# Attention and two MoE layers on one core: sums moved between engines, a shorter weight conversion, a new order

## The chip, the cores and the metric

One Trainium2 chip, one core. The metric is the device time of one execution in microseconds (us). A core has TensorE (PE in the profile), VectorE (DVE), ScalarE (ACT), GpSimd (POOL) and SyncE (SP), which here issues most DMAs. Each engine works through its own instructions in order and waits on semaphores.

## What is computed

Attention over q, k, v (batch 4, 8 heads, 576 tokens, 64 columns), then two feed-forward layers. Attention has two parts that are added:

```
q_d, k_d, v_d = mean over groups of 4 tokens            # 144 pooled tokens
out_up    = repeat(softmax(scale * q_d k_d^T) v_d, 4)   # pooled, for every token
out_local = softmax(where(|i - j| < 4, scale * q k^T, -1e9)) v
x = out_up + out_local                                  # 2304 tokens x 512
x = silu(x @ w_in) @ w_out                              # 512 -> 2048 -> 512
out = rational(x @ w_in2) @ w_out2                      # cubic over quadratic
```

Both softmaxes subtract the row's maximum and divide by the sum of the exponentials (+ 1e-9). The weights arrive as 64-bit floats, and the kernel converts them on the chip.

## The kernel before, in words

**Attention.** Each batch has five chunks of 116 or 112 tokens. A chunk's k and q, with a halo, come in one DMA (tile kq, six buffers), its v in another (vw). The local part of a chunk c of batch b is a row of jobs: S (scores with a band mask, L563, L572), M (maxima, L578), E (exponentials, L584 and eight L588), U (their sum L593, plus 1e-9 L594, reciprocal L595), N (scaling, L598, on VectorE or GpSimd), T (transposes, L609), C (copy to PT), O (times v, L629), A (add the pooled part, L636), H and X (split into a rounded half and a rest, L650). The pooled part runs in two halves: s, m, e (six L478), u (sum L483, reciprocal L484), n, t, c, o (L510), U. A needs its result, so the first chunk's x waits for the whole pooled part of its batch.

The sums over four tokens of q and k (tile kqd) and of v (vd) are made in two ways. In batch 0 five reductions on VectorE (job R, L399) read the kq tiles, and v comes in four strips (tile vst, L409) that GpSimd (L417, L418) or VectorE (L415) adds up. In batches 1 to 3 four DMAs per sum put the four tokens' parts on one another; the last three accumulate and are issued by GpSimd (L428, L435).

**The MoE layers.** The first layer runs in 80 steps: five blocks of some 460 tokens times 16 slices of the hidden width. Steps 0 to 7 are block 0 with slices 0 to 7, steps 8 to 23 block 1 with all slices, then the rest of block 0 and the other blocks. A step is twelve matmuls into the hidden layer (h_mm, L798), an activation (L961, L964, L334, L973), and twelve matmuls out of it (o_mm, L812). Each weight slice of both layers (64 pieces) is first converted by `piece`: 1 (absolute value of the high word, L710), 2 (the low word scaled, L714), 3 (clamp L717, then shift and mask L719), 4 (add, L723, on VectorE or GpSimd), 5 (sign and exponent, L726), 6 (rounded half), 7 (rest, L734). Steps 0 to 7 need 16 pieces, steps 8 to 15 none, steps 16 to 23 again 16; the second layer's 32 go to DRAM along the way. The second layer (from about 545 us) loads them back.

**The order.** Nothing is scheduled at run time. `Plan` holds every job of attention, conversion and the first layer with a due time, its cost on each engine that may do it, the jobs it comes after and the buffers it takes and gives back; `Plan.run` lists them by a simulation of the engines, latest start first, and each engine gets its instructions in that order. Jobs marked `port` don't run on VectorE and GpSimd at once. EARLY bounds how far ahead of its latest start a job may begin (50 us). `settle` repeats the simulation ROUNDS times with the start times that it found and keeps the best. While no MoE step has begun, gaps of TensorE are filled with matmuls that nothing reads (warm, L294).

Of the kernel before, what the change touches and what calls it, by code (L numbers as in the profile page):

```python
# [52 lines left out]
EARLY = 50000.0  # L53
ROUNDS = 6
WARM0 = 20
WARM0_END = 3800.0
# [20 lines left out]
class Job:  # L77
# [3 lines left out]
    def __init__(self, name, due, cost, emit, after=(), take=(), give=(), margin=0.0, size=0.0,  # L81
                 closes=False, early=EARLY, port=False, step=None):
        self.port = port
# [12 lines left out]
class Plan:  # L96


    LAT, OWN = 200.0, 90.0
    DMA_LAT = 2000.0  # L100
# [23 lines left out]
    def run(self, when):  # L124
# [20 lines left out]
        free = dict.fromkeys("PVAGD", 0.0)  # L145
        port = 0.0
# [4 lines left out]
        while events:  # L151
# [87 lines left out]
def v_ns(n):  # L239
    return 66 + 1.042 * n  # L240
# [10 lines left out]
def r_ns(n, count):  # L251

    return count * (n / 2.4 + 17)
# [3 lines left out]
def tile_kernel(ctx, tc, kq, kqs, vp, vw_in, moe_w_in, moe_w_out, moe2_w_in, moe2_w_out, moe2_a, moe2_b, out):  # L257
# [87 lines left out]
    E2_t = [at.tile([128, 6, SD + 1], F32, tag=f"EE{i}", name=f"EE{i}", bufs=1) for i in range(2)]  # L345
# [19 lines left out]
    for e in E2_t:  # L365
        nc.gpsimd.memset(e[:, :, SD:], 1e-9)
# [8 lines left out]
    def attention(b):  # L375
# [17 lines left out]
        vs = []  # L393
        if b == 0:
            for t in range(NCH):
                def sm(e, t=t):
                    o = kqd[:, :2 * KT * SD].rearrange("p (g s) -> p g s", g=2 * KT)[:, :, at0[t] // 4:(at0[t] + CHUNKS[t]) // 4]
                    i = kqt[t][:, :2 * KT * KW].rearrange("p (g s) -> p g s", g=2 * KT)[:, :, HALO:HALO + CHUNKS[t]]
                    nc.vector.tensor_reduce(out=o, in_=i.rearrange("p g (j r) -> p g j r", r=4), axis=AX.X, op=ALU.add)  # L399
                sums.append(plan.add(f"R{b}{t}", FAR, {"V": v_ns(8 * CHUNKS[t])}, sm, after=[loads[t]] + sums[:1],  # L400
                                     take=[] if sums else [kdu], give=[kqu[t]]))
            for i in range(2):
                for hf in range(2):
                    wn = 2 * i + hf + NF - 7
                    u = Unit(f"w{wn}")
                    st = {}
                    def lv(e, i=i, hf=hf, st=st, wn=wn):
                        st[0] = wp.tile([128, 4, 256], F32, tag=f"w{wn}", name="vst")[:HS]
                        nc.sync.dma_start(out=st[0], in_=vp[b, :, :, i, 256 * hf:256 * hf + 256].rearrange("r s c -> s r c"))  # L409
                    def pv(e, i=i, hf=hf, st=st):  # L410
                        if not vdt:
                            vdt[0] = at.tile([HS, 2, DM], F32, tag="vd", name="vd", bufs=1)
                        o = vdt[0][:, i, 256 * hf:256 * hf + 256]
                        if e == "V":
                            nc.vector.tensor_reduce(out=o, in_=st[0].rearrange("p r c -> p c r"), axis=AX.X, op=ALU.add)  # L415
                        else:
                            nc.gpsimd.tensor_tensor(out=st[0][:, 0:2], in0=st[0][:, 0:2], in1=st[0][:, 2:4], op=ALU.add)  # L417
                            nc.gpsimd.tensor_tensor(out=o, in0=st[0][:, 0], in1=st[0][:, 1], op=ALU.add)  # L418
                    l = plan.add(f"v{b}{i}{hf}", FAR, {"D": 60}, lv, take=[u], size=HS * 4096)
                    vs.append(plan.add(f"p{b}{i}{hf}", FAR, {"G": 2050, "V": 1950}, pv,  # L420
                                       after=[l] + vs[:1], take=[] if vs else [vdu], give=[u]))
        else:
            def ks(e, r):
                o = kqd[:, :2 * KT * SD]
                if r == 0:
                    nc.sync.dma_start(out=o, in_=kqs[b, r])
                else:
# [9 lines left out]
            for f, u, o, n, m in ((ks, kdu, sums, "K", 128 * 4608), (vsum, vdu, vs, "Q", HS * 4096)):  # L437
                j = None
                for r in range(4):
                    j = plan.add(f"{n}{b}{r}", FAR, {"G": 1000} if r else {"D": 60}, lambda e, f=f, r=r: f(e, r),  # L440
                                 after=[j] if j else takes[n], take=[] if j else [u], size=m, margin=500 if r else 0)
                    if r == 0:
                        takes[n] = [j]
                o.append(j)
        if b == 0:
            takes.update(K=sums[:1], Q=vs[:1])
# [4 lines left out]
        for m in range(2):  # L451
# [20 lines left out]
            def ex(e, x=x, eu=eu):  # L472
                x["e"] = E2_t[eu.no]
                nc.scalar.activation(x["n"], x["n"], AF.Copy, scale=D ** -0.5 / 16.0)
                for e_ in range(2):
                    for t in range(3):
                        i = 3 * e_ + t
                        nc.scalar.activation(x["e"][:, i, :SD], x["s"][:, e_, SD * t:SD * t + SD], AF.Exp,  # L478
                                             scale=D ** -0.5 / 16.0, bias=x["n"][:, i:i + 1])

            def su(e, x=x):
                x["r"] = at.tile([128, 6], F32, tag="r2", name="r2", bufs=3)
                nc.vector.tensor_reduce(out=x["r"], in_=x["e"], axis=AX.X, op=ALU.add)  # L483
# [47 lines left out]
            jo = plan.add(f"o{b}{m}", d0, {"P": 950}, pv2, after=pc + vs + ups[:1], take=[p3] + ([] if ups else [upu]), give=[pt, vdu],  # L531
                          margin=MARGIN if b else MARGIN0)
# [4 lines left out]
        for c in range(NCH):  # L537
# [44 lines left out]
            def ex(e, x=x, eu=eu):  # L582
                x["e"] = E_t[eu.no]
                nc.scalar.activation(x["n"], x["n"], AF.Copy, scale=D ** -0.5)  # L584
                for e_ in range(2):
                    for g in range(KT):
                        i = KT * e_ + g
                        nc.scalar.activation(x["e"][:, i], x["s"][:, e_, WK * g:WK * g + WK], AF.Exp,  # L588
                                             scale=D ** -0.5, bias=x["n"][:, i:i + 1])

            def su(e, x=x):
                x["r"] = at.tile([128, 8], F32, tag="r1", name="r1", bufs=4)
                nc.vector.tensor_reduce(out=x["r"], in_=x["e"], axis=AX.X, op=ALU.add)  # L593
# [58 lines left out]
            if i == 0:  # L652
# [4 lines left out]
            js = plan.add(f"S{b}{c}", d0, {"P": 1000}, s, after=[loads[c]], take=[pS, eu], give=[kqu[c]],  # L657
                          margin=MARGIN if b else MARGIN0)
            jm = plan.add(f"M{b}{c}", d0, {"V": v_ns(8 * WK)}, mx, after=[js])
            je = plan.add(f"E{b}{c}", d0, {"A": 8 * (a_ns(WK) + 93) + 200}, ex, after=[jm], give=[pS])  # L660
            ju = plan.add(f"U{b}{c}", d0, {"V": v_ns(8 * WK) + 270}, su, after=[je])
            jn = plan.add(f"N{b}{c}", d0, {"V": v_ns(8 * WK), "G": 130 + 1.72 * 8 * WK}, no, after=[ju], port=True)
            jt = plan.add(f"T{b}{c}", d0, {"P": 530}, tr, after=[jn], take=[pT] + ([] if b == 0 and c == 4 else [pt]), give=[eu],
                          margin=MARGIN if b else MARGIN0)
            jc = plan.add(f"C{b}{c}", d0, {"A": a_ns(8 * sub), "V": v_ns(8 * sub)}, cp_, after=[jt] + (c3 if b == 0 and c == 4 else []), give=[pT])
            c3 = [jc]
            jo = plan.add(f"O{b}{c}", d0, {"P": 770}, pv, after=[jc, jl] + ups, take=[pO, xu], give=[pt, vu],
                          margin=MARGIN if b else MARGIN0)
# [7 lines left out]
    takes = {}  # L676
# [13 lines left out]
    def piece(name, due, src, dst, home, after=None):  # L690
# [485 lines left out]
```

## Time and profile before

| | us |
|---|---|
| median of 3 runs | 924.31 (923.57 to 924.56) |
| the profiled execution, its time | 927.42 |
| its span, first to last instruction | 925.6 |
| TensorE busy | 898.1 |
| VectorE busy | 721.8 |
| ScalarE busy | 597.9 |
| GpSimd busy | 333.7 |
| granted TensorE clock, mean | 0.993 |

The profile is of one execution. A line as L717 is a line of the kernel before. A busy TensorE is not TensorE at its peak, since matmuls are pipelined and their ends modelled; so below its work is also counted in matmuls.

### The profile page before, as it was taken

The page shows a single profiled execution, that of the slowest core. Times are in us where ns is not written, and L with a number is a line of the kernel's source. Part 1 is how long each engine was busy: PE and PEld are TensorE (multiplying, and loading weights), DVE is VectorE, ACT ScalarE, POOL GpSimd, SP SyncE. Part 2 cuts the span into 40 slices and gives each one's busy share as a digit, 9 for nine tenths or more (in the row PEclk, how much of TensorE's full clock was granted, in tenths as well). Part 3 has the DMA queues.
Part 4 walks back from the last instruction along what each step waited for, and adds up shares of the span by engine and source line. Part 5 has one row for each costly group of instructions (what it writes and reads, how often), then busy time and mean ns, then how long its engine had stood idle before and what let it go on. Part 6 is the DMA issues. An engine that isn't in the chain of part 4 may idle for free.

```text
span 925.6 us, 15469 instructions
## 1 busy us (share of the span) xinstructions
PE 898.1 (97%) x5885; PEld 759.2 (82%) x5885; DVE 721.8 (78%) x1054; ACT 597.9 (65%) x1179; POOL 333.7 (36%) x271
## 2 busy tenths in 40 slices
PE   7898999999999999999999999999999999999997
PEld 5676788867887788888888878888888888898996
DVE  7998995997458757886322289998998899799995
ACT  5867664766447746664222378888777877788874
POOL 4532231523124312110000146565554555455553
PEclk9998999999999999999999999999999999999999
DMA  8997897788889787879864091002001100200000
GB/s 263 309 268 242 262 280 240 277 265 247 266 241 315 255 275 255 277 279 322 272 233 159 10 393 48 1 1 91 1 1 43 38 0 1 80 1 1 35 1 35
DMA packets 48614, 152.36 MB, mean 165 GB/s; under 512 B 5308, under 2 KB 10556, under 8 KB 48540
## 3 DMA queue, kind: packets, MB, share of 16 engines
q1 hardware_dynamic: 45548, 142.46, 44.4%
q0 software_dynamic: 2704, 8.91, 5.6%
q8 instruction: 46, 0.75, 0.3%
q14 instruction: 28, 0.23, 0.1%
q10 hardware_dynamic: 288, 0.00, 0.0%
HBM read 115.81 MB, written 35.55 MB: 164 GB/s over the span
## 4 chain that ended last, share of the span: by engine, by line
PE 80%; DVE 10%; ACT 3%; issue 3%; DMA 2%; POOL 1%; SPq 0%; POOLq 0%; DVEq 0%; ACTq 0%
PE hps L798 37%; PE acc L1047 21%; PE acc L812 18%; DMA kq<-kq 1%; DVE cw L719 1%; DVE cw L726 1%; DVE cw L717 1%; DVE cr L723 1%; DMA raw<-moe_w_in 1%; PE pair L629 1%; PE pair L510 1%; DVE r L593 1%; PE pair L572 1%; DVE xs L636 1%; DVE r L594 1%
## 5 line engine op out<-in xcount | busy, mean ns | idle before, releaser
L798 PE MATMUL hps<-xh,w 128*128 128x460 f32 (+1 forms) x640 | 221.6, 381 | 3.7 <-POOL w L734 1.4
L812 PE MATMUL acc<-gh,wo 128*128 128x460 f32 (+1 forms) x640 | 220.9, 378 | 1.4 <-ACT w L334 1.4
L885 POOL TENSOR_TENSOR u<-u,ah 128x512 f32<-128x512 f32 (+1 forms) x80 | 96.0, 1200 | 278.9 <-ACT u L883 275.6
L798 PE MATMUL hps<-x2h,wi 128*128 128x512 f32 (+1 forms) x640 | 196.4, 368 | 0.0
L1047 PE MATMUL acc<-wo,gh 128*128 128x512 f32 x576 | 178.0, 390 | 0.0
L798 PEld LDWEIGHTS hps<-xh,w 128*128 128x128 f32 x640 | 121.0, 190 | 21.4 <-ACT w L334 2.1
L812 PEld LDWEIGHTS acc<-gh,wo 128*128 128x128 f32 x640 | 120.4, 188 | 17.9 <-ACT w L334 1.8
L798 PEld LDWEIGHTS hps<-x2h,wi 128*128 128x128 f32 x640 | 118.8, 188 | 16.4
L1078 POOL TENSOR_TENSOR gl<-p,gh 128x512 fp32r<-128x512 f32 (+1 forms) x80 | 120.7, 1509 | 11.6 <-issue 8.9
L1047 PEld LDWEIGHTS acc<-wo,gh 128*128 128x128 f32 x576 | 107.6, 188 | 20.9
L798 PE MATMUL hps<-xl,w 128*128 128x460 f32 (+1 forms) x320 | 119.8, 374 | 0.5 <-DVE xl L650 0.5
L812 PE MATMUL acc<-gl,wo 128*128 128x460 f32 (+1 forms) x320 | 118.8, 371 | 0.0
L798 PE MATMUL hps<-x2l,wi 128*128 128x512 f32 (+1 forms) x320 | 117.7, 368 | 0.0
L964 DVE SCALAR_TENSOR_TENSOR th<-th,hps 128x460 f32<-128x460 f32 (+1 forms) x80 | 50.3, 628 | 82.9 <-ACT th L961 82.8
L1047 PE MATMUL acc<-wo,gl 128*128 128x512 f32 x288 | 112.8, 392 | 1.0 <-POOL gl L1078 1.0
L961 ACT ACTIVATE th<-hps 128x460 f32<-128x460 f32 (+1 forms) x80 | 44.7, 559 | 104.3 <-PE hps L798 103.4
L1070 DVE SCALAR_TENSOR_TENSOR u<-u,r 128x512 f32<-128x512 f32 (+1 forms) x80 | 99.4, 1243 | 2.8
L1063 ACT ACTIVATE r<-u,cst 128x512 f32<-128x512 f32 (+1 forms) x80 | 54.5, 682 | 56.5 <-POOL u L885 52.7
L1069 DVE SCALAR_TENSOR_TENSOR u<-u,r 128x512 f32<-128x512 f32 (+1 forms) x80 | 82.9, 1037 | 3.9 <-ACT r L1064 3.9
L973 DVE TENSOR_TENSOR gl<-th,gh 128x460 fp32r<-128x460 f32 (+1 forms) x77 | 53.3, 692 | 27.4 <-ACT gh L334 27.0
L882 DVE TENSOR_TENSOR p<-p,hps 128x512 f32<-128x512 f32 (+1 forms) x80 | 50.5, 631 | 30.1 <-ACT p L881 30.0
L334 ACT ACTIVATE gh<-th 128x460 fp32r<-128x460 f32 (+1 forms) x80 | 46.9, 587 | 39.9 <-DVE th L964 29.4
(125 smaller groups left out, 1445.9 us busy)
## 6 DMA issues: line engine op xcount, KB each, us to landing
wo<-wos SPq DMA_DIRECT2D x64, 512.0 KB, 5.8
raw<-moe_w_in SPq DMA_DIRECT2D x32, 512.0 KB, 6.5
raw<-moe_w_out SPq DMA_DIRECT2D x32, 512.0 KB, 5.3
w2s<-cvo SPq DMA_DIRECT2D x32, 512.0 KB, 3.8
kq<-kq SPq DMA_DIRECT2D x20, 496.0 KB, 9.1
wos<-wo SPq DMA_DIRECT2D x16, 512.0 KB, 3.7
wi<-w2s SPq DMA_DIRECT2D x16, 512.0 KB, 10.2
wo<-w2s SPq DMA_DIRECT2D x16, 512.0 KB, 6.3
```

Of the source, the lines that this page charges most:

```text
L334: nc.scalar.activation(out, in_, AF.Copy, scale=scale)
L798: nc.tensor.matmul(hps[:, :n], lhsT=wi[:, i, 128 * g:128 * g + 128], rhs=(a, b)[s][:, g, :n], start=(m == 0), stop=(m == len(mms) - 1))
L812: nc.tensor.matmul(acc_t[p][g // 2][:, g % 2, :n], lhsT=wo[:, i, 128 * g:128 * g + 128], rhs=s_[:, :n], start=(f == f0 and m % 3 == 0), st ...
L882: nc.vector.tensor_tensor(out=p, in0=p, in1=hps, op=ALU.mult)
L885: nc.gpsimd.tensor_tensor(out=u, in0=u, in1=ah, op=ALU.mult)
L964: nc.vector.scalar_tensor_tensor(out=x["t"][:, :n], in0=x["t"][:, :n], scalar=1.0, in1=x["h"][:, :n], op0=ALU.add, op1=ALU.mult)
L973: eng(e).tensor_tensor(out=gl_t[s][:, :n], in0=x["t"][:, :n], in1=gh_t[s][:, :n], op=ALU.subtract)
L1047: nc.tensor.matmul(acc2[j][c], lhsT=a[:, 128 * c:128 * c + 128], rhs=wo[:, i, :], start=(f == 0 and m % 3 == 0), stop=(f == NF - 1 and m % ...
L1063: nc.scalar.activation(r, u, AF.Ln, scale=2.0 ** -64, bias=cst[:, 0:1])
L1069: nc.vector.scalar_tensor_tensor(out=u, in0=u, scalar=1.000001, in1=r, op0=ALU.add, op1=ALU.mult)
L1070: nc.vector.scalar_tensor_tensor(out=u, in0=u, scalar=-2.0, in1=r, op0=ALU.add, op1=ALU.mult)
L1078: nc.gpsimd.tensor_tensor(out=gl2[k_][:, :n], in0=p, in1=gh2[k_][:, :n], op=ALU.subtract)
```

## The change

- Every exponential also writes the sum of its row (accum_out), in the local and the pooled part. The reductions over the exponentials are gone; the pooled half adds 1e-9 in an instruction of its own where an extra column held it before.
- The sums of q and k are made on VectorE from the kq tiles in every batch; the DMAs of kqs and that input are gone. The sums of v in batches 1 to 3 stay with the DMAs.
- The pooled v of batch 0 is made by TensorE from the vw tiles, which stay in their weight buffers: `pm` builds a matrix of ones from the identity on VectorE (a fill and twelve small reductions), `vpool` multiplies (24 matmuls of 256 columns), `vcopy` copies the result (two copies). The four strips are gone.
- In `piece`, step 3 is one instruction (multiply by 2^-112, minimum); step 4 shifts and joins on VectorE alone; the constants of steps 2 and 5 fit to that.
- The plan: new costs for TensorE's jobs and for a switch between attention and MoE on it, EARLY 20 us, two rounds, 60 ns more for each exponential, the DMA queue from 1.5 us on. What is emitted for a job is otherwise as before; the order is listed anew.

```diff
-EARLY = 50000.0
-ROUNDS = 6
+EARLY = 20000.0
+ROUNDS = 2
+ACC = 60.0
-WARM0_END = 3800.0
+WARM0_END = 5300.0
+FIRST = 1500.0
...
+    SWITCH = {(False, True): 90.0, (True, False): 195.0, (True, True): 0.0, (False, False): 0.0}
...
+                    if best == "P":
+                        free[best] += self.SWITCH[att, j.att]
+                        att = j.att
...
+        for t in range(NCH):
+            def sm(e, t=t):
...
+                nc.vector.tensor_reduce(out=o, in_=i.rearrange("p g (j r) -> p g j r", r=4), axis=AX.X, op=ALU.add)
+            sums.append(plan.add(f"R{b}{t}", FAR, {"V": v_ns(8 * CHUNKS[t])}, sm, after=[loads[t]] + (sums[:1] or takes.get("K", [])),
+                                 take=[] if sums else [kdu], give=[kqu[t]]))
...
+            def pm(e):
+                w = vpx["w"] = wp.tile([128, sum(PMW)], F32, tag=f"w{NF - 7}", name="pm")
+                nc.vector.memset(w, 0.0)
...
+                                nc.vector.tensor_reduce(out=w[r, pm_at(c, s_, j):pm_at(c, s_, j) + m],
+                                                        in_=ident[r, i0:i0 + n * m].rearrange("p (j r) -> p j r", r=n),
+                                                        axis=AX.X, op=ALU.add)
...
+            def vpool(e, c):
...
+                                nc.tensor.matmul(vpx[0][:HS, a, 256 * kk:256 * kk + 256], lhsT=vpx["w"][r, o:o + HS],
+                                                 rhs=v0t[c // 2][r, c % 2, s_].rearrange("p h d -> p (h d)"),
+                                                 start=s_ == 0 and lo <= HS * kk, stop=s_ == 1 and hi_ >= HS * (kk + 1))
+
+            def vcopy(e):
...
+                    copy(e, vdt[0].rearrange("p k (m a f) -> p a (k m) f", m=2, a=2)[:, a],
+                         vpx[0][:HS, a].rearrange("p (q f) -> p q f", q=4))
...
-            def ks(e, r):
-                o = kqd[:, :2 * KT * SD]
-                if r == 0:
-                    nc.sync.dma_start(out=o, in_=kqs[b, r])
-                else:
-                    nc.gpsimd.dma_start(out=o, in_=kqs[b, r], accum_op=ALU.add)
...
                         nc.scalar.activation(x["e"][:, i, :SD], x["s"][:, e_, SD * t:SD * t + SD], AF.Exp,
-                                             scale=D ** -0.5 / 16.0, bias=x["n"][:, i:i + 1])
+                                             scale=D ** -0.5 / 16.0, bias=x["n"][:, i:i + 1],
+                                             accum_out=x["r"][:, i:i + 1])
...
-                nc.vector.tensor_reduce(out=x["r"], in_=x["e"], axis=AX.X, op=ALU.add)
+                nc.vector.tensor_scalar(out=x["r"], in0=x["r"], scalar1=1e-9, scalar2=None, op0=ALU.add)
                 nc.vector.reciprocal(out=x["r"], in_=x["r"])
...
                         nc.scalar.activation(x["e"][:, i], x["s"][:, e_, WK * g:WK * g + WK], AF.Exp,
-                                             scale=D ** -0.5, bias=x["n"][:, i:i + 1])
+                                             scale=D ** -0.5, bias=x["n"][:, i:i + 1], accum_out=x["r"][:, i:i + 1])
...
+            if b == 0:
+                vjobs["p"][0].after.append(jl)
+                vjobs["p"][c].give.append(vu)
...
         def c3(e):
-            nc.vector.tensor_scalar(out=x["w"], in0=x["w"], scalar1=W_LOW, scalar2=W_HIGH, op0=ALU.max, op1=ALU.min)
-            wi = x["w"].bitcast(I32)
-            nc.vector.tensor_scalar(out=wi, in0=wi, scalar1=3, scalar2=0x3FFFFFFF,
-                                    op0=ALU.logical_shift_left, op1=ALU.bitwise_and)
+            nc.vector.tensor_scalar(out=x["w"], in0=x["w"], scalar1=2.0 ** -112, scalar2=W_HIGH * 2.0 ** -112,
+                                    op0=ALU.mult, op1=ALU.min)
 
         def c4(e):
-            eng(e).tensor_tensor(out=x["r"], in0=x["w"].bitcast(I32), in1=x["r"], op=ALU.add)
+            nc.vector.scalar_tensor_tensor(out=x["r"], in0=x["w"].bitcast(I32), scalar=3, in1=x["r"],
+                                           op0=ALU.logical_shift_left, op1=ALU.bitwise_or)
```

## Rows read from the trace of the kernel before

**Rows 1.** The page, TensorE: busy us, share, instructions.
```profile
PE 898.1 (97%) x5885; PEld 759.2 (82%) x5885; DVE 721.8 (78%) x1054; ACT 597.9 (65%) x1179; POOL 333.7 (36%) x271
```

**Rows 2.** Table by stage: length; busy PE, PEld, DVE, ACT, POOL; clock; DMA; GB/s.
```profile
8.00:46.00 38.00, 30.99 (x651) 23.75 (x651) 36.28 (x63) 31.41 (x105) 20.25 (x19) 1.00 0.99 310
46.00:105.00 59.00, 52.69 (x466) 40.58 (x456) 55.28 (x98) 40.66 (x88) 17.16 (x14) 0.94 0.84 254
105.00:180.00 75.00, 73.08 (x397) 64.44 (x396) 60.34 (x99) 43.91 (x88) 22.77 (x18) 1.00 0.85 269
180.00:205.00 25.00, 22.15 (x218) 17.32 (x217) 22.78 (x41) 17.75 (x50) 8.96 (x7) 0.93 0.80 259
```

**Rows 3.** The same table for line L294 (fillers) alone, the first 46 us.
```profile
0.00:46.00 46.00, 21.52 (x149) 14.23 (x149) 1.00 0.91 286
```

**Rows 4.** Timeline of PE: start, length, engine, line, operation.
```profile
46.07 0.47 PE L798 MATMUL hps<-xh,w 128*128 128x464 f32 x1
```

**Rows 5.** The chain of waits near 142 us: start, length, what.
```profile
142.59 1.88 PE hps L798 x9
```

**Rows 6.** The table by stage for L798, then L812, then attention's tile pair.
```profile
46.00:105.00 59.00, 26.09 (x97) 18.37 (x97) 0.94 0.84 254
105.00:410.00 305.00, 148.59 (x606) 112.37 (x606) 0.99 0.83 267
...
46.00:105.00 59.00, 18.44 (x75) 14.11 (x75) 0.94 0.84 254
105.00:410.00 305.00, 147.14 (x598) 109.64 (x597) 0.99 0.83 267
...
46.00:105.00 59.00, 10.98 (x294) 0.94 0.84 254
105.00:410.00 305.00, 38.91 (x1144) 0.99 0.83 267
```

**Rows 7.** Groups of 8 to 46 us: count, busy us, mean ns, idle before.
```profile
L593 DVE TENSOR_REDUCE r<-E 128x8 f32<-128x512 f32 x5 | 3.4, 672 | 0.2 <-ACT E L588 0.2
L483 DVE TENSOR_REDUCE r<-EE 128x6 f32<-128x870 f32 x2 | 2.1, 1044 | 0.0
L717 DVE TENSOR_SCALAR cw<-cw 128x512 f32<-128x512 f32 x5 | 2.9, 590 | 0.0
L719 DVE TENSOR_SCALAR cw<-cw 128x512 int32<-128x512 int32 x5 | 2.2, 432 | 0.2
L723 DVE CUSTOM_DVE_ANT_0 cr<-cw,cr 128x1024 uint16<-128x1024 uint16 x3 | 2.1, 684 | 0.0
L399 DVE TENSOR_REDUCE kqd<-kq 128x232 f32<-128x928 f32 x3 | 3.3, 1100 | 0.2 <-DMA kq<-kq 0.2
L415 DVE TENSOR_REDUCE vd<-vst 72x256 f32<-72x1024 f32 x1 | 1.9, 1912 | 0.0
L710 ACT ACTIVATE cw<-raw 128x512 f32<-128x512 f32 x6 | 4.2, 708 | 0.6 <-DVE w L734 0.6
```

**Rows 8.** Groups by line, 46 to 105 us.
```profile
L717 DVE TENSOR_SCALAR cw<-cw 128x512 f32<-128x512 f32 x12 | 6.2, 516 | 0.2 <-ACT cw L710 0.2
L719 DVE TENSOR_SCALAR cw<-cw 128x512 int32<-128x512 int32 x12 | 5.1, 427 | 0.4
```

**Rows 9.** Instructions in order of time on VectorE.
```profile
11.27 0.17 DVE L594 TENSOR_SCALAR r<-r 128x8 f32<-128x8 f32 x1
16.48 1.70 DVE L594 TENSOR_SCALAR r<-r 128x8 f32<-128x8 f32 x1
...
28.19 0.42 DVE L717 TENSOR_SCALAR cw<-cw 128x512 f32<-128x512 f32 x1
```

**Rows 10.** Instructions in order of time on ScalarE.
```profile
8.46 1.75 ACT L588 ACTIVATE E<-pair,n 128x64 f32<-128x64 f32 x8
...
19.62 1.74 ACT L478 ACTIVATE EE<-acc,n 128x144 f32<-128x144 f32 x6
```

**Rows 11.** Instructions in order of time on PE, first pooled output.
```profile
30.17 1.20 PE L510 MATMUL acc<-PT,vd 72*64 72x144 f32 x16
```

More of the change, by code (lines that the diff above doesn't have):

```diff
@@ L81, in __init__ @@
     def __init__(self, name, due, cost, emit, after=(), take=(), give=(), margin=0.0, size=0.0,
-                 closes=False, early=EARLY, port=False, step=None):
-        self.port = port
+                 closes=False, early=EARLY, port=False, step=None, att=False):
+        self.port, self.att = port, att
         self.closes, self.early, self.step = closes, early, step
@@ L145, in run @@
         free = dict.fromkeys("PVAGD", 0.0)
+        free["D"] = FIRST
+        att = True
         port = 0.0
@@ L251, in r_ns, with tile_kernel @@
 def r_ns(n, count):
-    return count * (n / 2.4 + 17)
+    return count * (n / 2.4 + (17.4 if n % 128 else 14.4))
 @with_exitstack
-def tile_kernel(ctx, tc, kq, kqs, vp, vw_in, moe_w_in, moe_w_out, moe2_w_in, moe2_w_out, moe2_a, moe2_b, out):
+def tile_kernel(ctx, tc, kq, vp, vw_in, moe_w_in, moe_w_out, moe2_w_in, moe2_w_out, moe2_a, moe2_b, out):
     nc = tc.nc
@@ L344, in tile_kernel @@
     E_t = [at.tile([128, 8, WK], F32, tag=f"E{i}", name=f"E{i}", bufs=1) for i in range(NE)]
-    E2_t = [at.tile([128, 6, SD + 1], F32, tag=f"EE{i}", name=f"EE{i}", bufs=1) for i in range(2)]
+    E2_t = [at.tile([128, 6, SD], F32, tag=f"EE{i}", name=f"EE{i}", bufs=1) for i in range(2)]
     kqd = at.tile([128, 2 * KT * SD + QPAD], F32, tag="kqd", name="kqd", bufs=1)
@@ L393, in attention @@
         vs = []
-        if b == 0:
[L395 to L415, printed above, removed]
-                        else:
[L417 to L421, printed above, removed]
-        else:
-            def ks(e, r):
-                o = kqd[:, :2 * KT * SD]
-                if r == 0:
-                    nc.sync.dma_start(out=o, in_=kqs[b, r])
-                else:
-                    nc.gpsimd.dma_start(out=o, in_=kqs[b, r], accum_op=ALU.add)
@@ L435, in vsum @@
                     nc.gpsimd.dma_start(out=vdt[0], in_=vp[b, r], accum_op=ALU.add)
[L437 to L446, printed above, removed]
+            j = None
+            for r in range(4):
+                j = plan.add(f"Q{b}{r}", FAR, {"G": 1000} if r else {"D": 60}, lambda e, r=r: vsum(e, r),
+                             after=[j] if j else takes["Q"], take=[] if j else [vdu], size=HS * 4096 * (2 if r else 1),
+                             margin=500 if r else 0)
+                if r == 0:
+                    takes["Q"] = [j]
+            vs.append(j)
         ups = []
@@ L525, in attention @@
             for e_, u in ((0, p1_), (1, p2)):
-                jt = plan.add(f"t{b}{m}{e_}", d0, {"P": 500}, lambda e, tr=tr, e_=e_, u=u: tr(e, e_=e_, u=u),
-                              after=[jn] + pt_[:1], take=[u] + ([pt] if e_ == 0 else []), give=[eu], margin=MARGIN if b else MARGIN0)
+                jt = plan.add(f"t{b}{m}{e_}", d0, {"P": 300}, lambda e, tr=tr, e_=e_, u=u: tr(e, e_=e_, u=u),
+                              after=[jn] + pt_[:1], take=[u] + ([pt] if e_ == 0 else []), give=[eu], margin=MARGIN if b else MARGIN0, att=True)
                 pt_.append(jt)
@@ L530, in attention @@
                                    lambda e, tc_=tc_, e_=e_: tc_(e, e_=e_), after=[jt] + pc[:1], give=[u]))
-            jo = plan.add(f"o{b}{m}", d0, {"P": 950}, pv2, after=pc + vs + ups[:1], take=[p3] + ([] if ups else [upu]), give=[pt, vdu],
-                          margin=MARGIN if b else MARGIN0)
+            jo = plan.add(f"o{b}{m}", d0, {"P": 1000}, pv2, after=pc + vs + ups[:1], take=[p3] + ([] if ups else [upu]), give=[pt, vdu],
+                          margin=MARGIN if b else MARGIN0, att=True)
             ups.append(plan.add(f"U{b}{m}", d0, {"A": a_ns(288), "V": v_ns(288)}, u2, after=[jo], give=[p3]))
@@ L583, in ex @@
                 x["e"] = E_t[eu.no]
+                x["r"] = at.tile([128, 8], F32, tag="r1", name="r1", bufs=4)
                 nc.scalar.activation(x["n"], x["n"], AF.Copy, scale=D ** -0.5)
@@ L738, in piece @@
         j2 = plan.add(f"{name}.2", FAR, {"A": 570}, c2, after=[j0], take=[iu])
-        j3 = plan.add(f"{name}.3", FAR, {"V": 850}, c3, after=[j1], port=True)
-        j4 = plan.add(f"{name}.4", FAR, {"V": 620, "G": 1270}, c4, after=[j2, j3], port=True)
+        j3 = plan.add(f"{name}.3", FAR, {"V": 430}, c3, after=[j1], port=True)
+        j4 = plan.add(f"{name}.4", FAR, {"V": 620}, c4, after=[j2, j3], port=True)
         j5 = plan.add(f"{name}.5", FAR, {"V": 620}, c5, after=[j4], give=[iu], port=True)
```

81 lines of the change are left out of this document (57 added, 24 removed).

## The prediction

> **What bounds the kernel now.** I read the page first: TensorE is busy 97% of the span [rows 1]. An average over stages with different limits says little, so the table by stage comes next [rows 2]. Before 8 us things only start up. From 8 to 46 us VectorE is busy 36.28 of 38.00 us, ScalarE 31.41 and the DMA engines 0.99, while TensorE runs attention of the first batch and 21.52 us of fillers [rows 3]. From 46 to 105 us VectorE is still busy 55.28 of 59.00; from 105 to 180 it idles 14.7 us and TensorE is full. The reader is to see that VectorE bounds the first 105 us and little of what follows.
>
> How much TensorE could give back is a second reading. The first hidden-layer matmul starts at 46.07 us [rows 4]. In steady flow nine of them take 1.88 us, 0.209 us each [rows 5]. I count the matmuls of both layers at that price and add the attention's busy time of the same stretch [rows 6]. From 46 to 105 us: (97 + 75) x 0.209 + 10.98 = 46.9, so 12.1 of 59 us are not work. From 105 to 410 us: (606 + 598) x 0.209 + 38.91 = 290.5, so 14.5 of 305. Some matmul records can be missing, so these are upper ends, and part of both is the alternation between attention and MoE itself. The granted clock averaged 0.94 in 46 to 105 and 0.93 in 180 to 205 us, 1.00 in the other stages [rows 2]: time at the lower level, behind gaps of TensorE, is inside these sums. So the prize is the head (46 us) and the eight hidden steps after it (97 matmuls, 12 a step).
>
> **The change, part by part.** Durations are those of the profiled execution (span 925.6 us, time 927.42); the three timed runs have a median of 924.31, so I carry the difference over to that.
>
> *Sums of the exponentials.* The reductions over them go: on VectorE 5 of 0.67 us and 2 of 1.04 in the head [rows 7], three and two more at the same prices in 46 to 105. In their place ScalarE writes one sum per exponential, 68 in the head (56 + 12), and each pooled half gets a small addition on VectorE, 0.17 us like L594 undisturbed [rows 9]: 0.35 in the head, 0.35 after. The trace has no such output. Below, it can cost nothing, since the exponential runs over the same columns anyway; less than nothing is excluded, as nothing leaves ScalarE there. Above, take one more instruction of one column: eight exponentials of 64 columns take 1.75 us, six of 144 take 1.74 [rows 10], so 0.219 and 0.290 each, 0.0009 a column and 0.162 fixed. I take half of the fixed part, 0.08, because the output fetches no operand: 5.4 us of ScalarE in the head.
>
> *Weight conversion.* The clamp L717 and the shift L719 become one instruction of the clamp's form, 0.42 us undisturbed [rows 9]. In the head 2.9 + 2.2 become 5 x 0.42, 3.0 gained [rows 7]; in 46 to 105, 6.2 + 5.1 become 12 x 0.42, 6.3 gained [rows 8]. The addition L723, which GpSimd did for 20 of 64 pieces, is now VectorE's alone, in the form of L726; at L723's 0.68 us on VectorE [rows 7], the one of the head costs 0.7 and the two of 46 to 105 cost 1.4.
>
> *Sums of q and k.* Batches 1 to 3 trade four DMAs each (three of them accumulating, issued by GpSimd) for five reductions of 1.10 us [rows 7]. Batch 1's fall in 46 to 105, before its pooled scores: 5.5 us of VectorE. They free GpSimd's and SP's queues. Each kq tile is now held until its sum is read, and the first sum waits for the pooled scores of the batch before; behind it on VectorE stand maxima and conversions of later chunks. With six kq buffers and the next batch's loads asked for early I cost this at nothing; with that cover gone it is a reduction late, 1.1 us.
>
> *Pooled v of batch 0.* GpSimd's additions, VectorE's 1.91 us [rows 7] and four strip loads go. In come a fill and twelve tiny reductions on VectorE: by columns alone (some 1,000 at 1.10/928) 1.2 us, with 0.17 for each of the 13 on top 3.4; I take 2.2, 13 x 0.17, as these rows are nearest. On TensorE come 24 matmuls of 256 columns; sixteen of 144 took 1.20 [rows 11], so 24 x 0.075 x 256/144 = 3.2 us, up to twice that since half as many run side by side: hidden by the fillers. ScalarE gets two copies of 512 columns, 0.162 + 512 x 0.0009 each, 1.2 us. The first of the matmuls now waits for all five vw tiles, and the whole in-order TensorE queue stands behind it: five kq and five vw are 3.8 MB, 12.3 us at this stage's 310 GB/s [rows 2], while the pooled output first used v at 30.17 us [rows 11]. That is cover enough.
>
> *Head, summed.* VectorE: -3.4 -2.1 -1.9 -3.0 +0.7 +0.35 +2.2; and L594 was held to 1.70 us once while GpSimd added v [rows 9], -1.5. That is -8.6: it could end at 36 us. ScalarE: 31.41 + 5.4 + 1.2 = 38.0. Of its eleven conversions there (L710, L714, 0.7 us each [rows 7]) the first hidden step needs two; nine, 6.3 us, may come later, which leaves 31.7 from 8 us on. So ScalarE is what is late next, and the first step starts at 40: **-6 us**, bounds -1 (little of the ahead work gives way) and -10 (VectorE's end). The DMA engines lose 1.2 MB of strips and three DMAs of 576 KB here, about 9 us at 310 GB/s, and cease to be full.
>
> *46 to 105.* VectorE: -2.0 -2.1 -6.3 +1.4 +5.5 +0.35 = -3.1. Over both stages 91.6 us become 79.9; at the old density (91.6 of 97) that takes 84.6, so step eight at 93, -12. TensorE's own 46.9 after a start at 40 would allow 87. I take 4 of the 12.1, **-4 us** (0 to -8), because the head's postponed conversions land here.
>
> *Later.* In 180 to 205 us VectorE is busy 22.78 of 25 [rows 2]; batch 2's sums join, the lighter conversions outweigh them. **-2 us** of the 14.5 (+2 to -4). The rest of the plan (costs of TensorE's jobs, two trial orders for six, work at most 20 us ahead, not 50) has no price of its own in the trace; rival 3 bounds it.
>
> Sum: -12. Span 913.6, its own time 915.4, the median **912.3 us**.
>
> *A rule against it.* L594 took 0.17 us alone and 1.70 with GpSimd at work, while the two reductions L483 averaged 1.04 [rows 7, 9]. The Trainium skill (SBUF — State Buffer, "Who interferes with whom") says that tensor_scalar can be held by a port pair that it shares with GpSimd, and that tensor_reduce on trn2 never is; the trace agrees. By the rule the change trades immune instructions for exposed ones: the four new additions before step eight at 1.70 would be +6.1, and the time 918; by undisturbed rows it stays 912.3. GpSimd loses work, so I keep the latter.
>
> **Rivals.**
> 1. *ScalarE becomes the bound* (slower). At 0.162 us a sum the head's ScalarE holds 31.41 + 11.0 + 1.2 = 43.6 us; if its order keeps the ahead work, the first step comes at 51.6, +5.6, of which 1 comes back: +5, **929**. It decides from (38.0 - 31.4 - 1.2)/68 = 0.08 us on. For it: ScalarE idles only 6.6 us there [rows 2]. Against: nine conversions can wait.
> 2. *Hidden anyway.* The 12.1 us are mostly alternation and in-order waits, and the head gains half: -3, **921**. For it: with VectorE 94% busy TensorE still shows 52.69 busy of 59 there [rows 2]. Against: a busy matmul may be a stalled one, as its clock of 0.94 says.
> 3. *Too little work ahead.* The 16 conversions of steps 0 to 7 left 12.1 us unused. If with 20 us of lead the 16 of steps 16 to 23 meet TensorE as the first did, 10 to 12 us are lost there, the -10 eaten: **924**. Against: VectorE idles 14.7 us just before.
> 4. *More comes.* -10, -8, -4: **902**.
>
> **How the numbers follow.** A measurement of this kernel tells 0.2%, 1.85 us, from no change. Forecast, 906 to 918: 0.56. Rival 4 (under 906): 0.06. Rival 2 (918 to 922.4): 0.15. Within 0.2%, mostly rival 3: 0.08. Slower: 0.15, rival 1 with 0.12 and a worse rival 3 with 0.03. So faster 0.77, same 0.08, slower 0.15. The range 902 to 925 leaves out rival 1, the worst of rival 3 and a little below.
>
> **What would show it.** The first hidden matmul at 40 us (right from 36 to 44), step eight near 95; VectorE's busy time from 8 us to step eight near 80; eight exponentials in 2.4 us, rival 1 if 3.0; the stretch after 545 us unchanged. The prediction is wrong if the first step doesn't move, or if its gain is lost before 410 us.

## The result, and the profile after

The changed kernel takes 913.87 us, the median of four runs (913.17 to 914.55), and the kernel before, on the same chip, 924.43 (923.57 to 925.03): a ratio of 0.9865 with a 95% interval of 0.984 to 0.989. The profiled execution took 914.33 us with a span of 912.6, against 927.42 and 925.6. The forecast was 912.3 in 902 to 925. The total came out; the way to it did not.

The page's line of busy times answers to [rows 1]. VectorE lost 25.9 us and GpSimd 59.6, ScalarE gained 13.4.

```profile
PE 898.5 (98%) x5927; PEld 761.3 (83%) x5927; DVE 695.9 (76%) x1040; ACT 611.3 (67%) x1379; POOL 274.1 (30%) x221
```

The table by stage of the kernel after (length; busy PE, PEld, DVE, ACT, POOL; clock; DMA; GB/s) answers to [rows 2]:

```profile
8.00:46.00 38.00, 34.12 (x659) 25.55 (x656) 32.79 (x58) 34.92 (x165) 6.51 (x6) 1.00 0.81 308
46.00:105.00 59.00, 57.31 (x532) 46.20 (x525) 50.16 (x96) 44.34 (x116) 13.21 (x11) 0.97 0.53 165
105.00:180.00 75.00, 75.00 (x390) 67.09 (x389) 57.02 (x96) 45.54 (x82) 6.72 (x6) 1.00 0.77 258
180.00:205.00 25.00, 24.07 (x245) 19.64 (x244) 20.04 (x38) 19.19 (x78) 4.90 (x4) 1.00 0.73 245
```

In the head ScalarE (34.92) is now busier than VectorE (32.79). From 46 to 105 us TensorE's busy time rises by 4.6 us, and in 180 to 205 us its clock is back at 1.00 (0.93 before).

The timeline of TensorE after has the first hidden-layer matmul, which answers to [rows 4], and the first of step eight, the first with 460 tokens:

```profile
52.44 0.48 PE L831 MATMUL hps<-xh,w 128*128 128x464 f32 x1
...
98.74 0.37 PE L831 MATMUL hps<-xh,w 128*128 128x460 f32 x1
```

Starts of hidden steps read so, in us:

| | first | step 8 | step 16 | step 64 | end of span |
|---|---|---|---|---|---|
| before | 46.07 | 104.86 | 145.55 | 437.68 | 925.6 |
| after | 52.44 | 98.74 | 136.97 | 425.19 | 912.6 |
| change | +6.4 | -6.1 | -8.6 | -12.5 | -13.0 |

The first step starts later and the eighth earlier. The span's -13.0 stands beside -10.6 between the medians, since the profiled execution of before lay 3.0 us above its median and that of after 0.5; so some 2.5 us of these differences can belong to that one execution of before. The table by stage for L831, then L845 (the two MoE matmul lines), 46 to 105 us, answers to [rows 6]: 114 + 84 matmuls instead of 97 + 75.

```profile
46.00:105.00 59.00, 27.46 (x114) 20.92 (x115) 0.97 0.53 165
...
46.00:105.00 59.00, 20.24 (x84) 15.38 (x84) 0.97 0.53 165
```

Why the first step is late stands in the chain of waits of the kernel after, 40 to 56 us (start, length, what; x12 is six exponentials with their six sums):

```profile
40.58 2.29 ACT EE L505 x12
...
43.00 2.49 ACT E L616 x16
...
48.14 2.29 ACT EE L505 x12
50.43 0.12 ACT xh L342
```

The two EE groups are the pooled exponentials of batch 1. In the new list its sums of q and k, its pooled scores (from 36.3 us; before, between 60 and 80 us) and these exponentials come ahead of the last xh of block 0, which stands behind them on ScalarE until 50.43 us. The head was not cut; work of a later stage was put into it.

### The profile page after: what moved, and what is told of

Read it like the earlier page. It is cut to its first block, busy times and chain, and to the rows that moved or that the text cites. A ratio compares the mean times of both kernels' runs of the same rounds, so it can differ in the third digit from the quotient of the medians.

```text
span 912.6 us, 15692 instructions
## 1 busy us (share of the span) xinstructions
PE 898.5 (98%) x5927; PEld 761.3 (83%) x5927; DVE 695.9 (76%) x1040; ACT 611.3 (67%) x1379; POOL 274.1 (30%) x221
## 4 chain that ended last, share of the span: by engine, by line
PE 86%; ACT 7%; DVE 4%; issue 1%; DMA 1%; ACTq 0%; DVEq 0%
PE hps L831 40%; PE acc L1080 22%; PE acc L845 21%; ACT E L616 3%; ACT EE L505 2%; DMA ab<-moe_b 1%; PE pair L537 1%; PE pair L655 1%; PE pair L599 1%; PE pair L635 1%; DVE n L494 0%; DVE EE L514 0%; DVE cr L755 0%; PE pair L523 0%; DVE xs L662 0%
## 5 line engine op out<-in xcount | busy, mean ns | idle before, releaser
L845 PE MATMUL acc<-gh,wo 128*128 128x460 f32 (+1 forms) x640 | 220.7, 377 | 0.0
L831 PE MATMUL hps<-xh,w 128*128 128x460 f32 (+1 forms) x640 | 220.0, 377 | 0.0
L831 PE MATMUL hps<-x2h,wi 128*128 128x512 f32 (+1 forms) x640 | 196.4, 368 | 0.0
L845 PEld LDWEIGHTS acc<-gh,wo 128*128 128x128 f32 x640 | 120.1, 188 | 16.0 <-issue 1.4
L831 PEld LDWEIGHTS hps<-xh,w 128*128 128x128 f32 x640 | 120.1, 188 | 15.6 <-issue 0.6
L831 PEld LDWEIGHTS hps<-x2h,wi 128*128 128x128 f32 x640 | 118.8, 188 | 16.4
L831 PE MATMUL hps<-xl,w 128*128 128x460 f32 (+1 forms) x320 | 119.0, 372 | 0.7 <-DVE xl L676 0.7
L845 PE MATMUL acc<-gl,wo 128*128 128x460 f32 (+1 forms) x320 | 118.4, 370 | 0.0
L831 PE MATMUL hps<-x2l,wi 128*128 128x512 f32 (+1 forms) x320 | 117.7, 368 | 0.0
L1006 DVE TENSOR_TENSOR gl<-th,gh 128x460 fp32r<-128x460 f32 (+1 forms) x72 | 47.8, 664 | 30.3 <-ACT gh L342 29.7
L342 ACT ACTIVATE gh<-th 128x460 fp32r<-128x460 f32 (+1 forms) x76 | 44.8, 590 | 35.9 <-DVE th L997 23.0
```

The lines of the kernel that those rows point to most:

```text
L342: nc.scalar.activation(out, in_, AF.Copy, scale=scale)
L831: nc.tensor.matmul(hps[:, :n], lhsT=wi[:, i, 128 * g:128 * g + 128], rhs=(a, b)[s][:, g, :n], start=(m == 0), stop=(m == len(mms) - 1))
L845: nc.tensor.matmul(acc_t[p][g // 2][:, g % 2, :n], lhsT=wo[:, i, 128 * g:128 * g + 128], rhs=s_[:, :n], start=(f == f0 and m % 3 == 0), st ...
L1006: eng(e).tensor_tensor(out=gl_t[s][:, :n], in0=x["t"][:, :n], in1=gh_t[s][:, :n], op=ALU.subtract)
```

## Experiments

The theory was that the work taken off VectorE while it bounds is the gain (W in the expectations). Its rivals: the gain comes from the order (letters with an O), either from the plan's new settings alone or from an order listed anew for the lighter work; and ScalarE takes back what VectorE gives. Ratios are to the kernel before on the same chip, with 95% intervals; the changed kernel's is 0.9865. The medians come from several chips, so versions are compared by their ratios.

### Work and settings, crossed

e1_old_plan: the work of the change, the plan's old settings.

```diff
-EARLY = 20000.0
+EARLY = 50000.0
-ROUNDS = 2
+ROUNDS = 6
...
-    SWITCH = {(False, True): 90.0, (True, False): 195.0, (True, True): 0.0, (False, False): 0.0}
+    SWITCH = {(False, True): 0.0, (True, False): 0.0, (True, True): 0.0, (False, False): 0.0}
...
```

> All of the change's work (sums by the exponentials, q and k sums on VectorE, v by TensorE, short conversion) with the plan's settings of before: work up to 50 us ahead, six trial orders, old costs of TensorE's jobs, no switch cost, DMA queue from 0. Theory W (the removed VectorE and DMA work buys the time): most of the gain stays, 914 to 918. Theory O (the new order buys it): 921 to 926.

e2_old_work: the work of before, the plan's new settings (the same lines the other way).

> The kernel before with nothing but the plan's new settings (20 us ahead, two trial orders, new TensorE costs, switch cost, DMA queue from 1.5 us). Theory W: 922 to 928, no gain without the work removed. Theory O: 913 to 918.

e1 took 912.13 us, 0.985 [0.9816, 0.9884]: as the changed kernel. e2 took 924.87, 0.9984 [0.9964, 1.0005]: as the kernel before. So the settings alone give nothing that can be measured, and this work has the gain under either. Each of these is a single order, though, and two orders of nearly the same work, e5 and e8 below, lose the whole gain. The start of the first step says nothing on it: e1 starts last of all, at 56.06 us, and has step eight at 97.49; e2 starts it at 48.22 and has step eight at 104.14.

### The same work in the old order

e14_before_order: the kernel before, every instruction in its own order, with sums from the exponentials, and the shorter conversion in the 44 of 64 pieces whose step 4 is VectorE's.

```diff
-                nc.vector.tensor_reduce(out=x["r"], in_=x["e"], axis=AX.X, op=ALU.add)
...
+                                             scale=D ** -0.5, bias=x["n"][:, i:i + 1], accum_out=x["r"][:, i:i + 1])
...
+            if j4.eng == "V":
+                nc.vector.tensor_scalar(out=x["w"], in0=x["w"], scalar1=2.0 ** -112, scalar2=W_HIGH * 2.0 ** -112,
+                                        op0=ALU.mult, op1=ALU.min)
+                return
```

> The kernel before in its own order and plan, with two of the change's edits alone: the exponentials write the sums (no reductions over them), and the conversion is the short one wherever VectorE does its addition (44 of 64 pieces; the other 20 stay as they were). q and k sums and pooled v as before. VectorE loses 22 + 18 us, ScalarE gains 15. Theory W (these two edits carry the gain, in whatever order): 8 to 13 us under before, 912 to 918 where before is 925. Rival O2 (the gain has to be harvested by a new listing): 0 to -4, 921 to 926.

It took 924.39 us, 0.9985 [0.9968, 1.0002]: nothing. Its table by stage:

```profile
8.00:46.00 38.00, 30.99 (x599) 22.91 (x600) 29.18 (x48) 33.88 (x159) 20.57 (x19) 0.91 0.92 287
46.00:105.00 59.00, 52.13 (x504) 40.50 (x503) 50.39 (x89) 44.75 (x121) 17.00 (x14) 1.00 0.88 264
```

Against [rows 2] VectorE is relieved of 7.1 + 4.9 = 12.0 us in these stages, as much as I had counted on, yet the first step starts at 48.95 (before 46.07) and step eight at 105.81 (before 104.86). Where the 12 us went is in what VectorE waits for, 8 to 105 us (engine, tile and line, what it waited for: us, times, longest). The kernel before:

```profile
DVE wo L734 <- ACT wo L334: 1.1, 1, 1.1
DVE w L734 <- ACT w L334: 0.6, 1, 0.6
...
DVE th L964 <- ACT th L961: 0.5, 1, 0.5
...
DVE cw L717 <- ACT cw L710: 0.2, 1, 0.2
DVE r L593 <- ACT E L588: 0.2, 1, 0.2
```

e14:

```profile
DVE r L594 <- ACT E L590: 3.9, 3, 2.6
DVE th L972 <- ACT th L969: 1.7, 2, 1.4
DVE cw L718 <- ACT cw L710: 1.4, 1, 1.4
...
DVE xl L650 <- ACT xh L335: 1.2, 1, 1.2
DVE w L742 <- ACT w L335: 1.1, 3, 0.6
...
DVE wo L742 <- ACT wo L335: 1.0, 1, 1.0
DVE r L484 <- ACT EE L480: 0.9, 1, 0.9
DVE gl L981 <- ACT gh L335: 0.9, 1, 0.9
```

Waits for ScalarE rise from 2.6 to 12.1 us: 9.5 us more, against the 12.0 that VectorE was relieved of. (Waits for TensorE, not shown, rise from 1.3 to 4.7.) In an order that was written for a busy VectorE, ScalarE is the next to be late. So W fell in its pure form: these two edits, the largest of the change, are worth nothing in the old order. Two things stay open. e14 also puts more work on ScalarE (78.6 us busy in these stages, 72.1 before), and no run separates that from the order. And no run lists these two edits anew without the sums of q, k and v, so which part of the new list harvests them is not shown. In the kernel after, VectorE waits 7.5 us for ScalarE in the same stretch:

```profile
...
DVE th L997 <- ACT th L994: 2.9, 4, 1.5
DVE r L510 <- ACT EE L505: 2.2, 2, 1.3
DVE gl L1006 <- ACT gh L342: 1.3, 2, 0.7
DVE r L620 <- ACT E L616: 1.1, 3, 0.6
```

### One engine at a time, in the new order

Four kernels hold the order of the kernel after and change only what some jobs emit. e3_conv_two gives every conversion a second VectorE instruction:

```diff
+            wi = x["w"].bitcast(I32)
+            nc.vector.tensor_scalar(out=wi, in0=wi, scalar1=0x7FFFFFFF, scalar2=None, op0=ALU.bitwise_and)
```

> The changed kernel in the changed kernel's own order, but each of the 64 conversions gets a second VectorE instruction over its 512 columns (an and-mask that alters nothing), as the conversion before had: 0.42 us each, some 17 of them (7 us) before step eight. Theory W: the first eight steps and the stretch to step 24 come later, +4 to +7, 918 to 921. If VectorE's load is hidden in the new order: under +1.5, 914 to 915.5.

e4_sums_dve gives the sums of the exponentials back to VectorE:

```diff
-                                             scale=D ** -0.5, bias=x["n"][:, i:i + 1], accum_out=x["r"][:, i:i + 1])
+                                             scale=D ** -0.5, bias=x["n"][:, i:i + 1])
...
+                nc.vector.tensor_reduce(out=x["r"], in_=x["e"], axis=AX.X, op=ALU.add)
```

> The changed kernel in its own order, but the exponentials write no sums and VectorE makes them by reductions as before (0.67 us a chunk, 1.04 us a pooled half; 22 us in all), while ScalarE loses 208 accumulator reads of some 0.075 us (15.6 us in all, 5 before the first step). Theory W (VectorE binds): +3 to +6, 917 to 920. Rival S (ScalarE's exponentials bind the new head, its chain to 54 us runs along them): -3 to +1, 911 to 915, and the first hidden step 2 to 4 us earlier.

e9_act_more puts a ScalarE instruction of one column, whose result nothing reads, behind each of batch 0's exponentials:

```diff
+                        if b == 0:
+                            nc.scalar.activation(fill[:, i:i + 1], x["n"][:, i:i + 1], AF.Copy)
```

> The changed kernel in its own order, with one more ScalarE instruction of one column behind each of the 52 exponentials of batch 0 (result unused): some 0.1 us each, 5 us of ScalarE, all before the first hidden step. Rival S (ScalarE is the bound of the stretch up to step eight): step eight and the end 4 to 5 us later, 918 to 919. Theory W (VectorE is): the first step later by 2 to 4, step eight by under 2, the end 914 to 916.

e10_no_eps leaves out the addition of 1e-9 to the sums (a sum is at least 1, so the float32 result is the same):

```diff
-                nc.vector.tensor_scalar(out=x["r"], in0=x["r"], scalar1=1e-9, scalar2=None, op0=ALU.add)
```

> The changed kernel in its own order without the addition of 1e-9 to the sums (each sum is at least 1, so in float32 the addition changes nothing): 28 VectorE instructions of 0.17 us less, 5.9 us with the gaps between them, some 2.5 before step eight, and as many places less at which GpSimd can hold VectorE. Theory W: -1 to -3, 911 to 913. If VectorE's load is hidden: 913.5 to 914.5.

The table by stage of e3, then of e9:

```profile
8.00:46.00 38.00, 33.16 (x622) 24.79 (x621) 32.88 (x61) 34.03 (x163) 6.71 (x6) 1.00 0.82 310
46.00:105.00 59.00, 53.46 (x523) 41.75 (x524) 55.87 (x106) 44.47 (x118) 12.38 (x11) 0.97 0.46 143
```
```profile
8.00:46.00 38.00, 31.35 (x554) 23.55 (x552) 27.87 (x49) 35.13 (x192) 5.98 (x6) 0.96 0.75 287
46.00:105.00 59.00, 56.59 (x599) 45.36 (x599) 53.87 (x102) 47.60 (x140) 13.72 (x12) 0.97 0.51 158
```

Busy time from 8 to 105 us and the start of step eight, each against the kernel after (VectorE 82.95, ScalarE 79.26, 98.74):

| | VectorE | ScalarE | step 8 | median us | ratio |
|---|---|---|---|---|---|
| e3_conv_two | +5.8 | -0.8 | +5.3 | 920.99 | 0.9951 [0.9936, 0.9965] |
| e4_sums_dve | +7.5 | -6.9 | +1.7 | 921.06 | 0.9932 [0.9907, 0.9958] |
| e9_act_more | -1.2 | +3.5 | +4.9 | 918.88 | 0.9934 [0.9915, 0.9952] |
| e10_no_eps | -2.2 | -0.5 | -2.1 | 911.55 | 0.9856 [0.9837, 0.9874] |

The reader is to see that in this order each engine is on the path: time put on VectorE alone moves step eight nearly one for one, time put on ScalarE no less (e9 adds 52 instructions of 0.09 us, 4.8 us), and e4, which takes from ScalarE and gives to VectorE, moves it little (it loses the rest later: step 64 starts 6.5 us behind the kernel after). The stages are cut at fixed times, so a busy time lacks what slid past 105 us; e9's lower VectorE is that. In this order e3 and e4 each give back about half of the gain or more (0.0086 and 0.0067 of 0.0135). e10's gain over the changed kernel is inside the intervals.

### Parts of the change, listed anew

e13_strips_old_plan and e8_strips make batch 0's pooled v from strips again; e13 with the plan's old settings, e8 with the new ones.

```diff
-            vpu, vpx, pmu = Unit("pair"), {}, Unit(f"w{NF - 7}")
...
+                        st[0] = wp.tile([128, 4, 256], F32, tag=f"w{wn}", name="vst")[:HS]
+                        nc.sync.dma_start(out=st[0], in_=vp[b, :, :, i, 256 * hf:256 * hf + 256].rearrange("r s c -> s r c"))
```

> Batch 0's pooled v from the strips again, listed with the plan's settings of before; against e1_old_plan. If e8_strips's +12 belongs to the strips: 920 to 926. If it was the listing (it lost its time after step 24, where no strip is left): 910 to 915.

> The changed kernel, but batch 0's pooled v comes from the four strips, added up by GpSimd and VectorE as before; order listed anew. It puts 1.9 us on VectorE and some 6 us on GpSimd back and takes 2 us of small VectorE instructions, 5.4 us of TensorE and 1.1 us of ScalarE away, all in the head. Theory W: nearly nothing, 913 to 916. If the head's GpSimd and DMA share were what counted: +3 or more, over 917.

e12_k_dma_old_plan and e5_k_dma make the sums of q and k of batches 1 to 3 by DMAs again, with old and new settings (e12 also charges an accumulating DMA once, as before, and not twice).

```diff
-        for t in range(NCH):
+        for t in range(NCH if b == 0 else 0):
...
+                    nc.gpsimd.dma_start(out=o, in_=kqs[b, r], accum_op=ALU.add)
```

> q and k sums of batches 1 to 3 by DMA again, this time listed with the plan's settings of before (as e1_old_plan, and with its single charge for an accumulating DMA); to be set against e1_old_plan (ratio 0.985 to before). If e5_k_dma's +15 belongs to the DMA sums: 920 to 928 again. If it was the listing that was unlucky, and VectorE's and the DMAs' way are worth the same: 910 to 914.

> The changed kernel, but batches 1 to 3 get their sums of q and k from DMAs as before (four each, three accumulating), its order listed anew: VectorE loses 15 reductions of 1.1 us, DMA and GpSimd's queue get 7 MB and nine issues back. Theory W as far as VectorE's load alone counts: a gain of up to 3, 911 to 914. Rival D (the DMA queues and their accumulation chains were the better part of the prize): +3 to +8, 917 to 922.

e11_old_plan_no_eps is e1 without the additions of 1e-9.

> e1_old_plan (the change's work, the settings of before) without the addition of 1e-9, in the same order as e1_old_plan: theory W, as in e10_no_eps: -1 to -3 from e1_old_plan, a ratio to before of 0.982 to 0.984, 908 to 910 where before is 925. If the gain of e10_no_eps was its order's own: 0.985.

| | median us | ratio |
|---|---|---|
| e13_strips_old_plan | 912.03 | 0.9846 [0.9826, 0.9867] |
| e8_strips | 926.53 | 1.0014 [1.0004, 1.0025] |
| e12_k_dma_old_plan | 915.59 | 0.9882 [0.9865, 0.99] |
| e5_k_dma | 929.58 | 1.0056 [1.0034, 1.0077] |
| e11_old_plan_no_eps | 911.16 | 0.9846 [0.9819, 0.9874] |

Under the old settings e13 equals e1, so pooled v on TensorE is worth nothing there, and e12 is 0.003 above e1 with overlapping intervals, some 3 us, if anything, for q and k. Under the new settings, leaving out either part costs the whole gain (for e5 more than either theory expected), which no price of theirs explains: in e8 the strips are over in the head, but TensorE is busy only 45.06 us at a clock of 0.93 between 250 and 300 us (e13: 50.00 at 1.00); in e5 it is 39.89 at 0.83 (e12: 50.00 at 1.00). Of the 14 us between the spans of each pair, e5 and e12 (927.8 and 914.2) lose most there, 10.1 us of it as idle TensorE; e8 and e13 (924.4 and 910.4) lose about half: by MoE matmuls begun, e13 leads by 20 at 250 us and by 50 at 300, and 30 x 0.209 = 6.3 us. The place can be seen in e5, in its table by stage:

```profile
265.00:270.00 5.00, 1.68 (x24) 1.50 (x28) 1.48 (x4) 3.15 (x18) 1.24 (x1) 0.52 0.99 306
270.00:275.00 5.00, 1.26 (x33) 0.81 (x32) 1.55 (x4) 2.50 (x13) 0.00 (x0) 0.50 0.63 117
275.00:280.00 5.00, 3.98 (x63) 3.07 (x56) 3.64 (x7) 1.49 (x7) 0.00 (x0) 0.50 0.77 256
280.00:285.00 5.00, 5.00 (x39) 4.06 (x38) 3.11 (x7) 3.72 (x17) 0.00 (x0) 0.77 0.24 66
```

and in its timeline of TensorE (in brackets the idle time ahead, and what ended it):

```profile
267.67 0.68 PE L652 MATMUL pair<-ident,E 58*128 58x58 f32 x8 [3.57 <-ACT E L633]
...
274.46 1.12 PE L672 MATMUL pair<-PT,vw 64*64 64x58 f32 x32 [3.74 <-ACT EE L522]
```

The list has TensorE at two attention jobs that ScalarE's exponentials hold up; it stands for 3.6 and 3.7 us with MoE matmuls queued behind (none starts between 262.2 and 278.2 us), and the granted clock falls to the lower level (0.50, 1.2 GHz) and is back at 1.00 only after 285 us. In e8 one such wait, 4.1 us ahead of the same kind of transpose, stands at 266.5 to 270.6 us with clock 0.50 behind it. In e12 and e13 TensorE waits for nothing there. So e5's bad list differs from the good one mainly by two long waits and the clock behind them, and one such wait with its clock makes up about half of e8's loss; the other half is spread and was not followed. Why the planner makes such a list under one setting and not the other stays open.

e11 is as fast as e1, so the additions of 1e-9 cost nothing in that order. No version clearly beats the changed kernel: the best ratios, 0.9846 twice, have intervals that hold 0.9865.

## Why the prediction came out

**Head, -6: failed.** The first step started at 52.44 us, +6.4; 36 to 44 us was to count as right. Two steps of the sum failed, both on ScalarE. It let nine of the eleven conversion instructions in the head give way; in the new list nine still run there, 6.2 us (groups of 8 to 46 us after):

```profile
L744 ACT ACTIVATE cw<-raw 128x512 f32<-128x512 f32 x5 | 3.5, 733 | 0.0
L748 ACT ACTIVATE cr<-raw 128x512 int32<-128x512 uint32 x4 | 2.7, 716 | 0.0
```

And it took the rest of the order as given, while the new list brought batch 1's pooled part in, with 2 x 2.29 us of exponentials. ScalarE is what is late there, as forecast: with less on it (e4) the first step starts at 50.49 us, with more (e9) at 55.06. VectorE counts too: relieved of the additions (e10), the step starts at 50.27. Rival 1's start of 51.6 came about, but not by its price of a sum, which is 0.095 us and not 0.162. Its conclusion fails with my step: the first start is no gauge of the time, as e1 shows.

**46 to 105, -4: mis-sized.** With some of batch 1's work already done, this stage gave 12.5 us (from +6.4 to -6.1). Some 1.8 us of it is clock, 0.94 before and 0.97 after: 0.03 x 59, an estimate that takes TensorE as busy in it. VectorE's busy time from 8 us to step eight was to be near 80; the table by stage after, cut at 98 us, has

```profile
8.00:98.00 90.00, 84.42 (x1142) 65.47 (x1140) 79.98 (x149) 76.77 (x277) 18.42 (x16) 0.98 0.65 224
```

so that part of the sum held, and step eight came at 98.74 rather than 95 since VectorE is no longer alone: ScalarE is at 76.77 of 90, and e9 shows that it counts. Head and stage together, -10 forecast, gave -6.1.

**Later, -2: mis-sized.** It was -6.9, of which 2.5 fell between steps 8 and 16 and 3.9 from there to step 64. A part of what came back is clock: by [rows 2] and the table after, (1.00 - 0.93) x 25 = 1.8 us in 180 to 205 us, an estimate of the same kind. What little was left after step 64 (0.5 us) agrees with "the stretch after 545 us unchanged".

**Sums of exponentials, 0.08 us each: near, 0.095.** ScalarE's timeline after, the start of eight exponentials and the instruction behind them:

```profile
8.59 0.32 ACT L616 ACTIVATE E<-pair,n 128x64 f32<-128x64 f32 x1
8.80 0.19 ACT L616 ACTIVATION_READ_ACCUMULATOR E<-pair,n 128x1 f32 x1
8.89 0.31 ACT L616 ACTIVATE E<-pair,n 128x64 f32<-128x64 f32 x1
...
10.93 0.24 ACT L612 ACTIVATE n<-n 128x8 f32<-128x8 f32 x1
```

Before, the eight of [rows 10] start at 8.46, and the instruction behind them is

```profile
10.04 0.26 ACT L584 ACTIVATE n<-n 128x8 f32<-128x8 f32 x1
```

From the first start to the instruction behind, the eight take 2.34 us after and 1.58 before, 0.095 more for each. The 1.75 us that the sum divided by eight runs to the end of the last exponential, which overlaps what follows: one costs 0.198 us, not 0.219. At 0.095 a sum is just over the 0.08 from which rival 1 was to decide.

**Conversion: right in price.** Groups of the head after, by line:

```profile
L755 DVE SCALAR_TENSOR_TENSOR cr<-cw,cr 128x512 int32<-128x512 int32 x4 | 2.7, 684 | 0.1
...
L751 DVE TENSOR_SCALAR cw<-cw 128x512 f32<-128x512 f32 x4 | 1.7, 417 | 0.0
...
L620 DVE TENSOR_SCALAR r<-r 128x8 f32<-128x8 f32 x5 | 0.9, 172 | 1.3 <-ACT E L616 1.1
...
L510 DVE TENSOR_SCALAR r<-r 128x6 f32<-128x6 f32 x2 | 0.3, 172 | 2.2 <-ACT EE L505 2.2
```

0.42 (L751) and 0.68 (L755), as costed; e3 shows that a price like it is paid nearly in full before step eight.

**Pooled v: hidden, as costed.** On VectorE the fill and the reductions, on TensorE the matmuls (48 recorded for the 24 issued), on ScalarE the copies; the first two lie ahead of 8 us, mostly where VectorE had waited 1.5 us for kq before:

```profile
4.51 0.42 DVE L413 MEMSET pm<- 128x432 f32 x1
4.96 1.40 DVE L425 TENSOR_REDUCE pm<-ident 64x14 f32<-64x56 f32 x12
```
```profile
22.18 5.41 PE L440 MATMUL acc<-vw,pm 64*72 64x256 f32 x48 [0.33 <-ACT EE L505]
```
```profile
27.63 1.08 ACT L342 ACTIVATE vd<-acc 72x512 f32<-72x512 f32 x2 [0.84 <-PE acc L440]
```

1.8, 5.4 and 1.1 us for 2.2, 3.2 (up to twice) and 1.2. **q and k:** the five reductions fell in the head (27 to 34 us), not in 46 to 105; a part of why the head grew.

**The rule against it.** The four new additions before step eight (L510, two of them in the group above) took 0.17, 0.17, 0.32 and 0.16 us, not 1.70. The additions L620 in the head took 172 ns, with GpSimd busy 6.51 us there; in e14's head, with GpSimd at 20.57, the same instruction averaged 814:

```profile
L594 DVE TENSOR_SCALAR r<-r 128x8 f32<-128x8 f32 x5 | 4.1, 814 | 3.9 <-ACT E L590 3.9
```

One of these five took 3.17 us, until 25.55 us, when a run of GpSimd's instructions had just ended (25.52); three took 0.16 to 0.17. In the kernel before two of five were held, for 1.70 and 1.27 us, where the sum counted one. The +6.1 did not come; the likely reason is that the change also emptied GpSimd (20.25 to 6.51 us busy in the head), which no run shows alone. The rule of the Trainium skill (SBUF — State Buffer, "Who interferes with whom") agrees with these rows.

**The other rivals.** Hidden anyway (2) is how e14 came out in the old order, but not the kernel as listed. Too little work ahead (3) had 20 us of lead as its cause; e1, with 50, is no faster. More (4) did not come.

So the sum of three terms that were each wrong, +6.4, -12.5 and -6.9 for -6, -4 and -2, came out at -13.0 for -12: that they add up is luck. What was right is the work removed and its order of size; what was missing is that a list made anew moves work between stages, which the forecast, stage by stage from the old list, left out.

## What to carry to other kernels

In a kernel whose instruction order is fixed, work taken off the busiest engine can turn into waits for the next one (in e14, 9.5 us of waits for 12.0 of relief) until the order is made anew for it: read the waits of the relieved engine before counting its time as gained. Compare two orders of the same work before judging a change that also makes a new order: here orders of the same work, made under two settings of the planner, lie up to 1.7% apart. Judge a start-up by when its last step is done, not by when the first begins.

## What the runs showed of the hardware

The sum output of an exponential is an instruction of its own on ScalarE (ACTIVATION_READ_ACCUMULATOR, 0.19 to 0.24 us long), yet back to back it costs only 0.095 us, since it overlaps the next exponential (it runs from 8.80 to 8.99 us, and that one starts at 8.89). A further one-column instruction behind each exponential (e9) costs 0.09, about as much: there the exponentials follow each other every 0.38 us, in the kernel after every 0.29.
